# Sparse attention with a gated unit behind it: dummy matmuls at the start, a bias loaded as rows, score strips by query halves, and a new order of work

## The chip, the cores and the metric

The kernel runs on one core of a Trainium2 chip. The core has five engines that work through queues of their own, in order: TensorE (PE) multiplies, VectorE (DVE) and ScalarE (ACT) do element-wise work and read TensorE's results out of PSUM, GpSimd (POOL) does element-wise work in SBUF only and issues casting DMAs, and SyncE (SP) issues DMAs. The metric is the device time of one execution in microseconds (us); shown is the median of several runs.

## The reference

Inputs are q, k and v of shape (4 batches, 8 heads, 768 positions, 64), and the weights of a gated unit. For every head:

```python
k_min, k_max = k_chunks.min(3), k_chunks.max(3)          # 24 chunks of 32 keys
ub = sum(maximum(q * k_min, q * k_max))                  # a bound per query and chunk
ub = where(causal, ub, -1e9)
top_chunks = argsort(ub)[..., -6:]                       # six chunks per query
scores = where(selected and causal, (q @ k.T) / 8, -1e9)
attn = softmax(scores) @ v
```

The heads of a batch are put side by side as x (768 x 512), and then:

```python
h = relu(x @ w_in);  u, v = h[:, :512], h[:, 512:]       # w_in: 512 x 1024
v_n = (v - mean(v)) / sqrt(var(v) + 1e-6)                # over the 512 features
v_s = w_spatial @ v_n + b_spatial[:, None]               # over the 768 positions
out = (u * v_s) @ w_out                                  # w_out: 512 x 512
```

## The kernel before

**Tiling.** Two heads make a pair; there are 16 pairs, four to a batch. Positions come in six tiles of 128. Data is fp16, sums in PSUM are fp32. Eight PSUM tiles of 128 x 512 fp32 (`bank0` to `bank7`) serve all matmuls.

**A pair's preparation** (`prep_ops`, and `prep_first` for pair 0, which goes head by head). Keys (`kp`) and queries (`qs`) are loaded by position; a load casts from fp32 to fp16 on the way when POOL issues it (L370), or goes to a `stage` tile by SP (L376) and is cast by an engine. Keys are transposed to `kT` by TensorE (L440, L545) or by a DMA that transposes (L443). VectorE reduces `kT` to the chunk maxima and negated minima `kmm` (L449 to L455, L552 to L560); these are spread to `km`, and the keys to `kh`. Queries are transposed on TensorE (L477, L579), and their positive and negative parts go to `rq`. The bounds are matmuls of `rq` with `km` (L489, L590); VectorE adds the causal mask, takes the eight largest (`max`), and writes into free columns of `qs` whether a chunk lies below the sixth (`select`). Transposing `qs` once more (TensorE L525 and L616, or DMA L516) gives `a`: 64 rows of queries and 24 rows of marks. Below the keys in `kh` stand 24 rows of -30000 (copies of `ex`), so that one matmul gives scores with the unselected chunks suppressed.

**A pair's attention** (`attend_ops`). For each head the scores stand with keys on partitions and queries along the row; the 21 causal blocks of 128 x 128 are put into six strips, groups of up to 512 columns (`STRIPS`). A strip is one or two matmuls (L641) into a PSUM tile, and ScalarE takes its exponential into `e` (L651). On the six diagonal blocks the triangle is cut off, either by a matmul that adds -30000 (L644) ahead of the exponential, or on GpSimd by two selects over three blocks each (L659) after it. Then 21 matmuls of 65 columns with the values and a column of ones (L667), a reciprocal (L675) and a product (L679) into `x16`, and a transposition of `x16` to `xT` (TensorE L694, or a DMA issued at L688).

**The gated unit of a batch** (`mlp_ops`). For each of six position tiles: v (L713), its statistics and normalization `vn`; u (L740); the spatial product (L754), which VectorE joins with the bias column `bcol` and with u to g (L758); g's transposition `gT` (TensorE L768, or DMA L762); the output product (L775), a copy to `o`, and a store by SP (L780). The bias column is loaded at L347 straight into the shape of 128 partitions x 6.

**What sets the order.** Every operation is registered with its choices of engine and with what it reads and writes, and then a written plan is played (`Schedule.run`): a string in which three characters stand for one operation, two for its number and one for the engine chosen and for the PSUM tile taken. So the order within each engine's queue, the engine of every copy, and the tile of every matmul are all fixed by that string. Where an operation exists in two forms (transposition by TensorE or by DMA, triangle by TensorE or GpSimd, load by POOL or by way of a stage), the plan lists only one of them. Buffers go round in rings (four tiles `e`, eleven `vraw`, four `o`, eight `stage`).

Of the kernel before, what the change touches and what calls it, by code (L numbers as in the profile page):

```python
# [10 lines left out]
Alu = mybir.AluOpType  # L11
# [9 lines left out]

STRIPS = [
    [(0, 0, 512, 0)],
    [(1, 128, 512, 0)],
    [(2, 256, 512, 0)],
    [(0, 512, 256, 0), (4, 512, 256, 256)],
    [(1, 640, 128, 0), (3, 384, 384, 128)],
    [(5, 640, 128, 0)],
]
WIDTHS = [512, 512, 512, 512, 512, 128]  # L30
BASES = [0, 512, 1024, 1536, 2048, 2560]
EW = 2688
DIAGS = [(0, 512), (1792, 384)]


def blocks(groups):
    out = []
    for g in groups:
        for (t, q0, n, col) in STRIPS[g]:
            for j in range(n // P):  # L40
                out.append((t, q0 // P + j, BASES[g] + col + j * P))
    return out
# [19 lines left out]
    "9wSBv0By0A909e49f06k06L0Ao16uWC907IO78G9mCCC06M0Db09x0Ay09n0De05GKCB0CJ15H16m4CK16n0A0873S6+CDP0"
    "Gg0CL4CG2CF26v0A107906/0IA07J0CI0CE2CM1Dg0CH1700CN0ABK740Di07SWCD1Gl0CO8BG47K07T0750DS0Dd0Df07A0"
    "9jC090710AC0BDOCP0720BH08/0CQ09k07cS9pG7B0Jg07d0BeKBE09q06w4Bf0CR0760GwC7e0AV0B887C07NO7fG6x0B90"
    "7707U0BJKBK07O0Bb4Bc0CS0Dh0AD07L0Gx0Dl29g0Dn1Dj2B2SB307D07g07h07P1Dr8Go07iWDk10Y0BTKDs09r0BQCBR0"
    "9h4BhOBi07j0Dt0A20B5S7Q0BW87V0Dq1Dm0DuG7E07k19s09t0Gz09u07F0Dv07W0A3CAE0Dw0IF0Dp1CmOAF0BU07R0Do1"
    "CjKB60Dx07M07G0II0G/0CYW7rSBX0Cn0IS0D84Ck0AG07l87m0DV0H71BL0CbO7s0BA0CpKCZ07oWBj07n0CeG7H0H91DB8"
    "Cc07X07Y0DC07t07p0Dy0HA1Cf0Cq0BBOBM0BY0AICHB87q07b0H10CwSB/08MGHC07uKH81AJ17Z0BZWG+07a00Z0Bk0Jy0"
    "8N0H00BN0Jo07v0H20HD1Bl0H60BO0D5CD90H317w07x0Cx0D08IU0H40Cz4EGS82OH50If1Cg0Bm0Cr0D60D10E8CC+0D20"
    "HEKHF0E908O0Ih8LA0HG0EH0E548CWE60IW08D0Ij1HH0E2C8E0EWSE30Jl0Ii0IT0EJ4EK0Ig18F0EeKIV0Ef0Ch8EQCED4"  # L70
    "EhWDD0HI0EE0Cs08P0BoKIY0830IX0EX0OW0Ct0840Ib0ETG8W4ER0J+0IZ0EbSEU0Ia1Ic1Ei0Id2Ec0K00850Bp1D3CDE0"
    "Jz0DF0IkGIl0LQW8X07y0EA0EBOJ/0DG0Im0K208Q0EL0EM0KBSIn0LI08Y0Cu0Ie1LR1EN0860K108gCKC1EO0HZKLU0Io0"
    "8h0Ha0HsWHt0DIGEY0Hm8Hn08i0Ej0EZOKA1HUKEk0I1WHV0LF0K50RW0LT0KD1DJ1K718Z0Ev8Ob0K42I20K61K928a0K30"
    "El0Em0LV07/4OmKLW0HcOEoS8j0LY0Hd0Gr0Ep0K81HpGLX0Lc0KEC8TWE+SHfOE/0On0Ew0Oq0FIKHq0IL0F00FJ0Lb0Ex0"
    "Oe0KF08U0KG0FDGF10800FE0Op0LhSFK0JR8HOWHg0Ey0HR4EqKHP0Er0HS0F20J3OKH0JUCH+WIu4FF1La0Es1Q00JJGJ40"
    "Ez0FVKKI0Et0JV0Hh0810Iv0FW0H/0Li0Ld1JS0FX0FbOFc0Lj0LZ0HxCHu0Hy0Eu0Q80JX4JK0FL0Os0Ou0JY0IxSOr0LkW"
    "Iy08d8FG0FhKLe18G0Fi0Lf0J9CJA0Ll0Ot0Jr0F30JMGF84HW0F90J6SLg1JN0Lm0HXCHi0Ow2T00I30Fj1FA1HvGJGKFH0"
    "Hj08e0Ln0Ov2FB0F40F50K+8QI0I40J70JZ0Rb0P14P20P30Hk0Oy1Fd0I+W8JSJH0O/189OO+1Lo0Oz18A1K/0FC0P01Ro0"
    "FM0F60Ox0I508K0Re0JO0I/0KcKL18Kp4KmSL20J00Kd0P4CFYWKq0I60Kf8KxOFZ0FSKP50Kn0KO4Fa1FT0FeGKy0KP08k0"
    "KRSQ50P60P70JB0KZOJPWF70FU08B0Ja0Jb0Kg0FN0Ka0Jc0Ks4MGKFO0L+8Kt0KS0FkCFf0Fg0MROLuWMS0J14FQ0MH0JC0"  # L80
    "KUSFP0Fl0M9GGCOFR0LxKGD0KV0Ku0QU1P80QJ0L/0Kh0QV1Fm0I70LL0QK0MUSKW0JD0MM8Rp0JE0Rq0Fn0GE0MA0L30Lv0"
    "QL0MN0QM0QN0Fo0GF0Rr0Rs0MV0MX4MY0Jd0M3GQT1MZ0M6WFuCKv8L40KXSL50T50M70PE4PF0QO0PfOFv0MJWL60Fw0Ly0"
    "Fx0Rt0M40Oh08n88o1Fy0QX4Ki0Kj0PiKS02QZ0GMGMK0M00QY1PSCPPWQQ0QP1GN0QW1Kk0M18Pg0PT0T80PV4PW0Ru0TI0"
    "PHOPI0PtSQS0MB0GO0MC0MD0ME08L0L70PqCPK4Pu0QR1Pj0GP0MO0MPOMa0PL0GWSRx2QaKPn8G24Pr0Rw2M+GPcCMb0Po0"
    "Pd0Mc0Md0Pv0N8OGX0GY0S18Qb0G30G40Qc0Qd0S30TK0TV18V0Rv2Pk0Qe0PQ0Ry1GZ0FrCRh0MlKFs0TJ0S20TXWTY0MqS"
    "S48MgCM/0TM0S50TL0S60TZ1R/2Mh0N00TN0S70QB0TO0TP0TS0Mm0Mn1Mo0Mi0N90NA1F/WNXGPX0NY08p0S80GG0Qq8TU2"
    "TQ1G00Mp0QnCG50Mj0Qr0Mr0GQ0TR0Ms0QyKQz0PlWG10TaOTb0Qk8Mt0Tc0Td0Q/4Pw0Px0Mu0NZ0TT1TE0NLSQo0PM0Mk0"
    "NIKN3GN40N51N60Ql0RCCRD0NJ0R+2N70RN8RO0NK1G60R00NM0QvONN0PNCQs0Mv0PY0Py0Qw0SfGGJ8Sg0St4Su0ScSNUK"
    "GK1R6OGa0Rz0Te0Sd0N10NV0NRWNS0GL0TF0Mw0My0R70TC0SKGR10Ft0PZ0Pa0SP8SS4SQ0SL0SnSSo0NW1NOONP0SECSF0"
    "RK8NQ1RHGR9KQtSNB0RI0R20GTOSiCR30N20RA0Mx0R40SqGRL0GdKRE0NC0Sr0ND0Sj0RP0G98ST0GU18f0NE0Ge1TnSTo0"  # L90
    "GA0SVGMz0NF0RFOTqCOMKTW1U64SW0SHSSI0NT1RQ0Tr0Na8SM0Nb0TkGTl0Ts0UCWTySU70NkCUD0Nl0NG0Sk0NH0Pz0Nc0"
    "U9GTz0Sv0T/4RR0RS0Nm0UA0UNOSX0Nn0NuWRT0Nd0No0U00SNSSY0SZ0TD0UKGUL0UO0Ne0UH4SlCSw0Sa0Nv0Tv8O2GUI0"
    "UP0Sx0Sy0Tw0Sz0ON0OO0U10Nw0TtOVNSU20U30U40Gf0UE0UF4UQ0UR0US0Nx0Ny0NrCNs0OP0UW8O30UUOUg4UV1UqCUvW"
    "O40Uh0O50UbKU+OUi1U/0V00Uj0Uk0UX0VBGV10V20Nt0UY0Uc0UZ0GB0Uw0Ux1VH4VI0Ud0Ue0Ur0Us0Uf0Ua0Ut0Uu0Uy0"
    "VJ0VKOUl0VO0Um0VP0OC8NhKUz0O60Ni0V8WUn0N/CUo0OQ0V30V40V60V90OD0GV0V70V50VL0O94OA1VC0OB0VuSVQKOE0"
    "VE4O00VA0O10Up0Vv0VR0VS0OF0VT0OTCVD0VM0VaWVb0Vc0Vd0Nj0Vw0VkGOG0VF0Vl0Vx0OU0Vm0VU0OV0Ve0OJOVG1Vn0"
    "W28W30Vy0W40WCKWD0WE0VhCW50WF0OK0Vo0OL0VXWW60WHSV/4Vi0WI0Vj0VrGVY0W00VZ0W10Vs0Vt0WJOWK0WL0W98WA0"
    "WB0"
# [3 lines left out]
class Bank:  # L102
    def __init__(self, cls):
        self.cls, self.tile = cls, None
# [14 lines left out]
class Schedule:  # L119
# [3 lines left out]
    def __init__(self, banks, caps):  # L123
        self.ops, self.banks, self.caps = [], banks, caps
        self.keys, self.mode = {}, {}

    def op(self, alts, emit, key, r=(), w=(), take=None, drop=None, load=0.0, tag="", when=None, after=()):
# [66 lines left out]
def kernel(  # L194
# [39 lines left out]
    pp = ctx.enter_context(tc.psum_pool(name="psum", bufs=1))  # L234
    banks = [pp.tile([P, 512], F32, name=f"bank{j}") for j in range(8)]
    s = Schedule(banks, {"sc": 3, "tr": 2, "ub": 1, "av": 2, "mlp": 4})
# [34 lines left out]
    bcol = cp.tile([P, NQT], F32, name="bcol")  # L271
    w_in_sb = cp.tile([P, NDO, DFF], F16, name="w_in")
# [7 lines left out]
    stage_r = ring(8, [P, NQT, D], F32, "stage")  # L280
# [10 lines left out]
    e_r = ring(4, [P, EW], F16, "e")  # L291
    rec_r = ring(4, [P, NQT, 1], F32, "rec")
    x_r = ring(3, [P, NQT, 2, D], F16, "x16")
    xT_r = ring(3, [P, NDO, S], F16, "xT")
    vr_r = ring(11, [P, DH], F32, "vraw")
# [7 lines left out]
    o_r = ring(4, [P, DM], F32, "o")  # L303

    nc.scalar.preload_act_table_set("natural_log_exp_and_others")
# [9 lines left out]

    def preset(qs):
        nc.vector.memset(qs[:, :, 0, 0:D], 0.0)
        nc.vector.memset(qs[:, :, 1, D:P], 0.0)

    def const_ops():  # L320
        s.op(("DVE", 0.1, 0.2), lambda: nc.vector.memset(identity, 0.0), -100, w=["identity"])
        s.op(("POOL", *pool(P)), c_identity, -100.95, w=["identity"], r=["identity"])
        for j in range(2):
            s.op(("DVE", 0.1, 0.2), lambda j=j: nc.vector.memset(km0[j], 0.0), -96 + j, w=[("km0z", j)])
# [298 lines left out]
    def attend_ops(i, key):  # L623
# [3 lines left out]
        for hi in range(2):  # L627
# [6 lines left out]
            for part in range(2):  # L634
                for g in range(3 * part, 3 * part + 3):
                    bs = Bank("sc")

                    def score(g=g, bs=bs, hi=hi, af=af, tri=False):
                        for (t, q0, n, col) in STRIPS[g]:
# [3 lines left out]
                            if dg:  # L643
                                mm(bs.f32[:, col:col + P], lhsT=identity, rhs=tri_t, start=False, stop=True)  # L644
# [185 lines left out]
```

## Time and profile before

| | |
|---|---|
| median of 6 runs | 196.69 us (196.08 to 198.28) |
| profiled execution | 196.08 us, of which the span from first to last instruction is 194.1 us |
| granted TensorE clock | 0.998 |
| TensorE matmuls | 1888, busy 180.8 us (93% of the span) |
| VectorE, ScalarE, GpSimd busy | 159.1, 147.7, 118.3 us |
| exponentials (L651) | 192, of which 160 have 512 columns (613 ns each) and 32 have 128 (298 ns) |
| triangles on GpSimd (L659) / TensorE (L644) | 48, 552 ns each / 48 matmuls |
| DMA | 29.5 MB, 122457 packets |

A row of the profile names a line of the kernel, an engine, an operation, what it writes and reads, how often, its busy time and its mean length. An arrow in brackets names what ended the idle time ahead of it. In the rows by stretches, each engine's busy time is followed by its number of instructions, and after the engines come the granted clock, the DMA engines' share and GB/s. Matmuls overlap in a pipeline, so a busy TensorE isn't one at its highest rate.

### The profile page before, as it was taken

The page shows a single profiled execution, that of the slowest core. Times are in us where ns is not written, and L with a number is a line of the kernel's source. Part 1 is how long each engine was busy: PE and PEld are TensorE (multiplying, and loading weights), DVE is VectorE, ACT ScalarE, POOL GpSimd, SP SyncE. Part 2 cuts the span into 40 slices and gives each one's busy share as a digit, 9 for nine tenths or more (in the row PEclk, how much of TensorE's full clock was granted, in tenths as well). Part 3 has the DMA queues.
Part 4 walks back from the last instruction along what each step waited for, and adds up shares of the span by engine and source line. Part 5 has one row for each costly group of instructions (what it writes and reads, how often), then busy time and mean ns, then how long its engine had stood idle before and what let it go on. Part 6 is the DMA issues. An engine that isn't in the chain of part 4 may idle for free.

```text
span 194.1 us, 5292 instructions
## 1 busy us (share of the span) xinstructions
PE 180.8 (93%) x1888; PEld 112.8 (58%) x1888; DVE 159.1 (82%) x568; ACT 147.7 (76%) x317; POOL 118.3 (61%) x207
## 2 busy tenths in 40 slices
PE   0579999999997999999999999999999999999992
PEld 0367888885664656565566566555565664444440
DVE  8799999997999789998999986799889436983620
ACT  7799999999996999778989978667888722652142
POOL 8699999999999798697976785523213530000000
PEclk9999999999999999999999999999999999999999
DMA  6999999999999999999999999799793264406565
GB/s 140 136 158 167 190 164 153 148 141 171 155 155 170 133 105 164 134 156 137 214 163 151 194 105 156 186 140 215 154 258 71 41 149 137 109 0 198 139 204 216
DMA packets 122457, 29.50 MB, mean 152 GB/s; under 512 B 117056, under 2 KB 119360, under 8 KB 122432
## 3 DMA queue, kind: packets, MB, share of 16 engines
q0 software_dynamic: 72528, 11.60, 93.5%
q1 hardware_dynamic: 49904, 17.57, 46.5%
q8 instruction: 14, 0.23, 0.5%
q14 instruction: 11, 0.09, 0.2%
HBM read 24.38 MB, written 6.29 MB: 158 GB/s over the span
## 4 chain that ended last, share of the span: by engine, by line
PE 73%; ACT 10%; DVE 7%; DMA 6%; issue 1%; SPq 1%; ACTq 0%; DVEq 0%
PE bank L641 15%; PE bank L754 13%; PE bank L775 10%; PE bank L740 9%; PE bank L667 9%; PE bank L713 8%; ACT e L651 4%; DMA a<-qs 4%; DMA stage<-in_k_dram 2%; PE bank L477 2%; ACT rq L250 1%; PE bank L489 1%; ACT kT L240 1%; PE bank L694 1%; ACT kh L240 1%
## 5 line engine op out<-in xcount | busy, mean ns | idle before, releaser
L651 ACT ACTIVATE e<-bank 128x512 f16<-128x512 f32 (+1 forms) x192 | 92.3, 561 | 12.6 <-PE bank L641 10.2
L641 PE MATMUL bank<-a,kh 128*128 128x512 f16 (+3 forms) x256 | 56.1, 305 | 1.1 <-DMA a<-qs 1.0
L659 POOL TENSOR_SCALAR_AFFINE_SELECT e<-e 128x384 f16<-128x384 f16 x48 | 25.7, 552 | 22.5 <-ACT e L651 21.5
L754 PE MATMUL bank<-vn,wsT 128*128 128x512 f16 x144 | 38.0, 379 | 0.0
L641 PEld LDWEIGHTS <-kh 128*128 128x128 f16 x256 | 22.7, 98 | 16.2 <-DMA a<-qs 1.2
L667 PEld LDWEIGHTS <-e 128*128 128x128 f16 x672 | 25.4, 97 | 5.0 <-issue 0.3
L667 PE MATMUL bank<-vt,e 128*128 128x65 f16 x672 | 27.1, 193 | 0.2 <-ACT e L651 0.2
L740 PE MATMUL bank<-w_in,xT 128*128 128x512 f16 x96 | 25.9, 379 | 0.0
L242 POOL COPY kh<-kT 64x384 f16<-64x384 f16 x46 | 24.0, 521 | 3.2 <-PE bank L641 1.3
L758 DVE SCALAR_TENSOR_TENSOR g<-bank,bcol,u 128x512 f16<-128x512 f32 x24 | 17.6, 745 | 10.1 <-PE bank L754 9.9
L370 POOL DMA_DIRECT2D qs<-in_q_dram x30 | 25.0, 836 | 0.0
L713 PE MATMUL bank<-w_in,xT 128*128 128x512 f16 x96 | 24.4, 379 | 0.0
L240 ACT COPY o<-bank 128x512 f32<-128x512 f32 x18 | 10.4, 587 | 18.3 <-PE bank L775 18.3
L775 PE MATMUL bank<-w_out,gT 128*128 128x512 f16 x96 | 23.6, 379 | 0.0
L754 PEld LDWEIGHTS <-wsT 128*128 128x128 f16 x144 | 13.4, 98 | 12.1
L679 DVE TENSOR_TENSOR x<-bank,rec 128x384 f16<-128x384 f32 x32 | 17.4, 547 | 0.4
L370 POOL DMA_DIRECT2D kp<-in_k_dram x15 | 15.5, 1032 | 2.1 <-ACT qs L240 1.5
L719 DVE BATCH_NORM_STATS2 st<-vraw 128x6 f32<-128x512 f32 x24 | 16.3, 684 | 0.4
L370 POOL DMA_DIRECT2D vt<-in_v_dram x15 | 15.4, 1025 | 0.0
L775 PEld LDWEIGHTS <-gT 128*128 128x128 f16 x96 | 9.1, 98 | 9.8
L713 PEld LDWEIGHTS <-xT 128*128 128x128 f16 x96 | 9.0, 98 | 9.0
L740 PEld LDWEIGHTS <-xT 128*128 128x128 f16 x96 | 8.9, 98 | 8.5
(90 smaller groups left out, 280.2 us busy)
## 6 DMA issues: line engine op xcount, KB each, us to landing
out_dram<-o SPq DMA_DIRECT2D x24, 256.0 KB, 2.3
kp<-in_k_dram POOLq DMA_DIRECT2D x15, 192.0 KB, 6.4
qs<-in_q_dram POOLq DMA_DIRECT2D x30, 96.0 KB, 5.6
vt<-in_v_dram POOLq DMA_DIRECT2D x15, 192.0 KB, 6.5
ws_raw<-in_moe_w_spatial_dram POOLq DMA_DIRECT2D x3, 384.0 KB, 6.2
w_in<-in_moe_w_in_dram POOLq DMA_DIRECT2D x4, 256.0 KB, 7.3
w_out<-in_moe_w_out_dram POOLq DMA_DIRECT2D x2, 256.0 KB, 6.0
stage<-in_k_dram SPq DMA_DIRECT2D x2, 192.0 KB, 3.4
```

Of the source, the lines that this page charges most:

```text
L242: nc.gpsimd.tensor_copy(o, f)
L370: s.op(("POOL", cost, 0), lambda: nc.gpsimd.dma_start(out=o[0] if len(o) == 1 else o[2], in_=f[0] if len(f) == 1 else f[2]), key, w=w, loa ...
L641: mm(bs.f32[:, col:col + n], lhsT=kh[:, hi, t * P:(t + 1) * P], rhs=af[:, q0 // P:(q0 + n) // P, :], start=True, stop=not dg)
L651: s.op(("ACT", *act_cost(WIDTHS[g])), lambda g=g, bs=bs, e=e: nc.scalar.activation(out=e[:, BASES[g]:BASES[g] + WIDTHS[g]], in_=bs.f32[:, ...
L659: nc.gpsimd.affine_select(out=o, in_=o, compare_op=Alu.is_ge, fill=0.0, base=0, channel_multiplier=-1, pattern=[[0, 3], [1, P]])
L667: mm(o[:, qi, :], lhsT=e[:, c:c + P], rhs=vt[:, hi, t, 0:D + 1], start=(part == 0 and n == 0), stop=(part == 1 and n == len(bl) - 1))
L679: nc.vector.tensor_tensor(x16[:, :, hi, :], in0=o[:, :, 0:D], in1=rec.to_broadcast([P, NQT, D]), op=Alu.mult)
L713: mm(bk.f32, lhsT=x[:, ko, t * P:(t + 1) * P], rhs=w_in_sb[:, ko, DH:DFF], start=(ko == 0), stop=(ko == NDO - 1))
L740: mm(bk.f32, lhsT=x[:, ko, t * P:(t + 1) * P], rhs=w_in_sb[:, ko, 0:DH], start=(ko == 0), stop=(ko == NDO - 1))
L754: mm(bk.f32, lhsT=wsT[:, si, t * P:(t + 1) * P], rhs=vn[:, si, :], start=(si == 0), stop=(si == NQT - 1))
L758: s.op(("DVE", 0.67, 0.80), lambda t=t, bk=bk, g=g: nc.vector.scalar_tensor_tensor(out=g, in0=bk.f32, scalar=bcol[:, t:t + 1], in1=u_r[nu[ ...
L775: mm(bo.f32, lhsT=gT[:, db, :], rhs=w_out_sb[:, db, :], start=(db == 0), stop=(db == KO - 1))
```

## The change

- **Dummy matmuls.** A zeroed tile `warm` is multiplied with itself in four groups (31, 5, 5 and 5 matmuls of 128 columns). The groups stand in the plan ahead of, and between, the key and query transpositions of pair 0.
- **Spatial bias.** The vector is loaded as six rows of 128 (`braw`), transposed on TensorE with a small fp32 identity `idf`, and copied to `bcol`.
- **Score strips.** The six groups hold the same 21 blocks but are ordered by query halves: two groups for the queries 0 to 383, four for 384 to 767. Each half has its own `e` tile (768 and 1920 columns, rings of four). A group now has one to three matmuls, 12 per head where there were 8. The values are multiplied after a half's groups: 6 blocks, then 15.
- **Triangles.** Each half's three diagonal blocks are cut on GpSimd as before or on VectorE, by a minimum with a 0/60000 tile `tri_m`. TensorE remains as a choice.
- **Loads.** Only k and q of pair 0 may go by way of a stage. The plan uses that for the first head's k and q.
- **Rings.** `vraw` nine, `o` three, `stage` four, `rec` eight.
- **PSUM.** Eight single tiles, as before (`double` is None). A variant that splits whole pairs into halves is written but set to zero (`SPLIT = 0`).
- **The plan** is a new string. Before / after it runs: key transpositions on TensorE 12 / 13 (of 17, pair 0's two heads counted apart); `a` on TensorE 10 / 10; x 7 / 6; g 1 / 5; triangles of eight heads on TensorE in both; the other 48 on GpSimd 48 / 40, on VectorE 0 / 8.

```diff
 STRIPS = [
-    [(0, 0, 512, 0)],
-    [(1, 128, 512, 0)],
-    [(2, 256, 512, 0)],
-    [(0, 512, 256, 0), (4, 512, 256, 256)],
-    [(1, 640, 128, 0), (3, 384, 384, 128)],
-    [(5, 640, 128, 0)],
+    [(0, 0, 256, 0), (2, 256, 128, 256), (0, 256, 128, 384)],
+    [(1, 128, 256, 0)],
+    [(0, 384, 384, 0), (5, 640, 128, 384)],
+    [(1, 384, 384, 0), (4, 512, 128, 384)],
+    [(2, 384, 384, 0), (3, 384, 128, 384)],
+    [(3, 512, 256, 0), (4, 640, 128, 256)],
 ]
-WIDTHS = [512, 512, 512, 512, 512, 128]
-BASES = [0, 512, 1024, 1536, 2048, 2560]
-EW = 2688
-DIAGS = [(0, 512), (1792, 384)]
+HALF = [(0, 2), (2, 6)]
+WIDTHS = [512, 256, 512, 512, 512, 384]
+BASES = [0, 512, 0, 512, 1024, 1536]
+EW = [768, 1920]
+DIAGS = [(0, 256), (384, 512)]
...
-    stage_r = ring(8, [P, NQT, D], F32, "stage")
+    stage_r = ring(4, [P, NQT, D], F32, "stage")
...
-    e_r = ring(4, [P, EW], F16, "e")
-    rec_r = ring(4, [P, NQT, 1], F32, "rec")
+    e_r = [ring(4, [P, n], F16, f"e{h}_") for h, n in enumerate(EW)]
+    rec_r = ring(8, [P, NQT, 1], F32, "rec")
...
-    vr_r = ring(11, [P, DH], F32, "vraw")
+    vr_r = ring(9, [P, DH], F32, "vraw")
...
-    o_r = ring(4, [P, DM], F32, "o")
+    o_r = ring(3, [P, DM], F32, "o")
...
+        s.op(("DVE", 0.08, 0.15), lambda: nc.vector.memset(warm, 0.0), -102, w=["warm"])
+        for j in range(NWARM):
+            bw = Bank("tr")
+
+            def spin(n=31 if j == 0 else 5, bw=bw):
+                for _ in range(n):
+                    nc.tensor.matmul(bw.f32[:, 0:P], lhsT=warm, rhs=warm, start=True, stop=True)
...
+        s.op(("DVE", 0.13, 0.25), lambda: nc.vector.tensor_scalar(
+            tri_m, in0=tri_t, scalar1=0.0, scalar2=60000.0, op0=Alu.is_ge, op1=Alu.mult), -30, r=["tri"], w=["trim"])
...
-        s.op(("SP", 0.45, 2.5), lambda: nc.sync.dma_start(out=bcol, in_=moe_b_spatial.rearrange("(t p) -> p t", p=P)),
-             20, w=["bcol"])
+        s.op(("SP", 0.45, 0), lambda: nc.sync.dma_start(out=braw, in_=moe_b_spatial.rearrange("(t p) -> t p", p=P)),
+             -60, w=["braw"], load=0.1, tag="lb")
...
+        s.op(("PE", 0.25, 0.47), lambda: nc.tensor.transpose(bb.f32[:, 0:NQT], braw, idf), 20, r=["braw", "idf"], w=[bb], take=bb)
...
-            cast, stage = s.choice(("ld", name, i))
+            cast = None
+            if i == 0 and name != "v":
+                cast, stage = s.choice(("ld", name, i))
...
+                def tri(eng, c0=c0, st=st, e=e):
                     o = bass.AP(e.tensor, e.offset + c0, [list(e.ap[0]), [st, 3], [1, P]])
-                    nc.gpsimd.affine_select(out=o, in_=o, compare_op=Alu.is_ge, fill=0.0, base=0,
-                                            channel_multiplier=-1, pattern=[[0, 3], [1, P]])
+                    if eng == "DVE":
+                        nc.vector.tensor_tensor(o, in0=o, in1=tri_m.unsqueeze(1).to_broadcast([P, 3, P]), op=Alu.min)
+                    else:
+                        nc.gpsimd.affine_select(out=o, in_=o, compare_op=Alu.is_ge, fill=0.0, base=0,
+                                                channel_multiplier=-1, pattern=[[0, 3], [1, P]])
```

## The prediction

> **What bounds the kernel now.** I read the page's totals and slices, then stretches of the run, the timeline of the start, the chain that ended last, and the groups by shape. From the page:
>
> ```profile
> PE 180.8 (93%) x1888; PEld 112.8 (58%) x1888; DVE 159.1 (82%) x568; ACT 147.7 (76%) x317; POOL 118.3 (61%) x207
> ...
> PE   0579999999997999999999999999999999999992
> ```
>
> TensorE (PE) has gaps only in the first three slices (4.9 us each), in one slice near 60 us and at the end. Busy time counts overlapped latencies, so I take TensorE's demand from dense pieces of the chain (start, length, work, count):
>
> ```profile
> 28.29 0.34 PE bank L525 x6
> ...
> 153.80 0.65 PE bank L667 x21
> ...
> 182.43 2.59 PE bank L754 x12
> ```
>
> That is 56 ns per 128-column transposition, 31 ns per 65-column matmul with the values, 216 ns per 512-column matmul. Priced so, the 1888 matmuls need: gated unit 432 x 216 = 93.3; scores 32 heads x 2688 columns = 36.5; values 672 x 31 = 20.8; 310 transpositions 17.4; 48 triangles 2.7; 170 small bound matmuls 4.3; together 175 us. The last matmul ends at 190.5, so 15.5 us are lost. Before 16.0 us only 60 transpositions and 20 bound matmuls ran, 3.9 us at these rates: 12.1 us are lost there. The other 3.4 lie later: 1.2 between 16 and 24 us, and then one visible stall plus about 1.1 in small pieces.
>
> The start, by stretches (length, then busy us of PE, PEld, DVE, ACT, POOL):
>
> ```profile
> 4.00:6.00 2.00, 0.50 (x3) 0.24 (x3) 1.65 (x6) 0.57 (x2) 1.92 (x3) 1.00 1.46 192
> 6.00:8.00 2.00, 1.32 (x9) 0.79 (x9) 1.10 (x7) 1.96 (x5) 0.59 (x1) 1.00 1.94 106
> 8.00:16.00 8.00, 6.35 (x69) 5.72 (x70) 7.66 (x43) 7.78 (x17) 7.91 (x11) 1.00 2.09 163
> 16.00:24.00 8.00, 7.78 (x116) 6.19 (x115) 7.58 (x41) 8.00 (x17) 7.57 (x18) 1.00 1.83 178
> ```
>
> From 8 us VectorE (DVE) and ScalarE (ACT) are full; TensorE waits for them. Only around 5 to 7 us do both have holes: they wait for the second head's keys. The timeline shows that, and the one later stall:
>
> ```profile
> 5.79 0.51 ACT L240 CAST kp<-stage 128x384 f16<-128x384 f32 x1 [1.43 <-DMA stage<-in_k_dram]
> ...
> 6.89 0.36 DVE L244 COPY kT<-bank 128x384 f16<-128x384 f16 x1 [1.14 <-PE bank L545]
> ...
> 7.15 0.82 PE L579 MATMUL bank<-identity,qs 128*128 128x128 f16 x6 [0.29 <-ACT qs L240]
> ...
> 17.11 1.08 ACT L651 ACTIVATE e<-bank 128x512 f16<-128x512 f32 x2
> ```
>
> ```profile
> 59.35 0.83 PE L641 MATMUL bank<-a,kh 128*128 128x128 f16 x5 [1.04 <-DMA a<-qs]
> ```
>
> The first exponential starts at 17.11. At 59.35 scores of pair 5 waited for their transposition by DMA, which the chain shows as 7.22 us long.
>
> [...] six transpositions took 0.82 us at 7.15 and pace at 0.34 later. [...] The column bias load agrees: 3 KB held SP's queue for 1.10 us and took 5.6 us to land.
>
> **The change part by part.** The plan string can be read by hand with Schedule.run's rule (two characters number the operation, the third gives engine and bank); counts below come from that.
>
> Dummy matmuls: 31 + 5 + 5 + 5 of 128 columns, cold at some 105 ns (six transpositions in 0.82 us, one lasting 0.31). The first 36 run from about 1.05 to 4.9 us, where TensorE has nothing else; the cast of k0 ended at 4.36, so they delay the first transposition by up to 0.5 us, which VectorE's queue covers (below). They may bring full speed by about 5 us, so a step of six transpositions ends some 0.3 us sooner; three such steps are in the first pair's chain. Later gaps may cool the array again: worth 0 to 0.9, inside the ramp below.
>
> Loads: k1 and q1 of pair 0 move from SP to POOL's casting queue; SP's two other stages, and a value load of pair 15, go. A new wait: in TensorE's queue the second head's key transposition waits for k1, and behind it stand the first head's queries, pair 1's keys and everything after. k1's issue follows the identity on POOL, at about 1.46. The shortest staged landing gives 3.05 us (0.80 to 3.85), the median key load before 16 us gives 6.1: it lands between 4.5 and 7.6. I take 6.0, since it is half as large and first in its queue; before, the staged one came at 5.79.
>
> The ramp, walked with the rows' durations: from ex (ends 2.1) VectorE has presets, memsets and three ex copies, 3.6 us, ahead of the first key copy, so that starts at 5.75 and finds its input. Reductions, second key copy (7.3 to 7.7), its reductions, pair 1's key copy, the queries' positive and negative parts (rq) follow without a hole: bounds at 10.4, select at 12.4. ScalarE is then in its own queue (copies, rq parts, key halves) and copies the first head's a at 13.5 to 14.3; four small copies and a key copy (0.8 + 0.8) stand before the first exponential, at 15.9. Before: 17.11, so 1.2 sooner; the second head's a, on VectorE, ends 16.3 against 17.2, 0.9 sooner. Work queued on ScalarE and VectorE ahead of TensorE's tenth us of work is equal in both plans (about 20 and 23.5 us), so the lead lasts: minus 1.0. Bounds: 0 (k1 late, or ScalarE's extra copies ahead of pair 2) to minus 2.5 (VectorE has 2 us less ahead of TensorE's twelfth us).
>
> Bias rows: SP's 1.10 becomes about 0.5; one small transposition, one copy of six columns: 0.1 us on engines; free, hidden by the bound chain; without cover 0.1.
>
> Score strips: the same 2688 columns per head and six exponentials, ScalarE's columns unchanged, but 12 matmuls instead of 8: 128 more x 2.7 ns = 0.35 us on TensorE, all on the path. Values are taken after two groups, then four; same 21 matmuls.
>
> Triangles: the same eight heads keep theirs on TensorE (48). Of 48 on GpSimd 8 move to VectorE, priced by the nearest row, a 128x384 f16 minimum over keys, 421 ns: 3.4 us there, 4.4 off GpSimd. VectorE's queue after 24 us has slack only in total (it is 97% busy to 44 us), but the first moved one is pair 4's. I take 0; 0 to 0.5.
>
> Re-planned transpositions: five gated tiles on TensorE instead of one, 4 x 4 x 56 = 0.9 us; keys 13 instead of 12, x 6 instead of 7: nothing. TensorE's sum: 0.35 + 0.9 + 0.05 = plus 1.3.
>
> The stall at 59: between pair 5's select and its first score the old plan leaves 7.2 us of TensorE work, the new one 9.1; against 7.22 us for the transfer that removes the stall: minus 1.3 (1.04 shown idle and the slower pieces at its sides). Next late is the shortest other distance: pair 13's 5.5 us, where before 5.4 ran without a stall; I take 0 for new ones, 0 to 1.5. Smaller rings (vraw 9, o 3): the last stores land 2.3 us after issue, and the plan keeps 4.7 us between tiles that share a buffer: 0, up to 0.3. "Eight PSUM tiles" is what was there. The end is again three output tiles, a copy and a store.
>
> Sum: -1.0 - 1.3 + 1.3 = -1.0. Profiled execution 196.08 (span 194.1, 1.98 around it) becomes 195.1; the median of the runs lies 0.6 above it, so 195.7. A measurement of this kernel can tell about 1% from no change.
>
> **The rivals.** Warm ramp in full: VectorE's hole and its 2 us of deferred work both count, -2.5; and the longer distances remove 0.7 of the small losses: 196.7 - 2.5 - 1.3 - 0.7 + 1.3 = 193.5. For: all transposition distances grew at the low end; against: ScalarE, as full as VectorE, has nothing less to do.
>
> Late second head (slower): k1 by POOL lands at 7.6 instead of 6.0. TensorE's queue is in order, so bounds and scores of both heads come 1.3 us later than before instead of 1.0 sooner; and a new late transfer takes back the stall (0 instead of -1.3): 196.7 + 1.3 + 1.3 = 199.3. It decides once k1 lands later than about 7.0. For: loads took 6.1 us here; against: those were twice as large and behind four staged loads.
>
> No warming: the array stays cold until dense work begins; the ramp gains 0.5 only: 196.2.
>
> **How the numbers follow.** Chances: forecast 0.38 (spread 1 us), no warming 0.10, warm ramp 0.33, late head 0.19. Faster by over 1% (below 194.7): 0.33 and 0.06 of the forecast's spread, 0.39; slower (above 198.7): 0.19; within 1%: 0.42. The range 193.0 to 199.0 leaves out the lower part of the warm ramp (0.08) and the upper of the late head (0.12).
>
> **What would show it.** Right: the first exponential near 16 us; 0.34 us paces for six transpositions by 7 us; no DVE hole at 5 to 7; no wait on the a transposition near 59; 1.3 us more TensorE work. Wrong: TensorE waiting on kp after 7 us, a ScalarE-bound stretch to 30 us with more loss than 1.2, or a new DMA wait in the middle.

## The result, and the profile after

The changed kernel takes 195.9 us in the median of 35 runs (194.6 to 198.5), beside 197.2 us of the kernel before on the same chips: a ratio of 0.9946, with an interval of 0.9927 to 0.9966. The forecast was 195.7 us and "within 1%". The profiled execution took 195.07 us, of which the span is 193.3.

The page of the kernel after, totals (busy time, share of the span, instructions), TensorE's slices and its granted clock:

```profile
PE 185.1 (96%) x2079; PEld 124.7 (65%) x2079; DVE 160.8 (83%) x575; ACT 149.8 (77%) x326; POOL 115.6 (60%) x198
...
PE   7689999899999999999999999999999999999992
...
PEclk9969999999999999999999999999999999999999
```

The dip of before at 59 us is gone, and the first slice is full, of dummies. The third digit of the clock is new: the granted clock was 0.50 from 10.44 to 13.86 us, most of that slice.

I price TensorE's matmuls much as in the prediction: columns / 2.4 plus 2.7 ns, the straight line through its measured 216 ns at 512 columns and 56 at 128 (these are from start to start; one such matmul lasts 379 and 219 ns in the profile); 30 ns for the 65 columns of a value matmul and 25.5 ns for a bound matmul, their paces in the profile; dummies at nothing. "Loss" at time T is T less the demand of all matmuls started by then. The demand is 175.7 us, before 174.4. The table says where the loss arises, in single profiled executions of both kernels and of all experiments below.

```
us lost by   16 us   24    36    56    60   100   180
before        11.9  12.9  13.0  13.2  14.5  15.3  15.8
after         10.8  11.8  12.7  12.8  12.8  13.5  13.6
e1_no_dummies 10.5  11.7  14.0  16.5  16.6  18.3  18.6
e2            11.9  13.3  13.2  13.4  14.9  15.9  16.2
e3            12.0  13.6  13.6  14.1  15.0  20.5  22.8
e4            10.7  11.6  12.6  12.6  12.7  13.2  13.6
e5            11.4  12.1  12.2  12.3  12.5  15.9  16.0
e6            11.0  12.1  12.3  12.3  12.3  13.0  13.2
e7            10.4  12.0  12.4  13.0  13.1  13.7  14.1
e9            10.2  11.2  11.4  11.4  12.4  12.7  13.0
e10           10.7  11.4  11.6  12.0  12.5  13.2  14.1
e11           11.1  12.1  12.2  13.4  13.3  14.7  14.9
e12           12.1  13.8  13.8  13.8  13.8  15.8  17.9
e15           10.7  11.4  13.5  13.4  13.5  16.1  16.2
```

So the kernel after is 1.1 us ahead at 16 us, gives back 0.6 by 56, gains 1.2 at 59, and 0.4 in small pieces after that: 2.1 us less lost at 180 us, 2.0 at the end, 1.27 us more to do, 0.8 us in all (span 194.1 to 193.3). Some executions of every kernel are slower than the rest: the medians given are of all executions, the ratios leave the slow ones out, and the profiles of e1 and e3 are of slow ones.

The timeline of the start, after (start, length, engine, line, work, count; in brackets the idle time ahead and what ended it):

```profile
1.05 4.02 PE L337 MATMUL bank<-warm 128*128 128x128 f16 x36 [1.05 <-DVE warm L331]
...
5.72 0.53 PE L573 MATMUL bank<-identity,kp 128*128 128x128 f16 x3
6.04 0.85 PE L607 MATMUL bank<-identity,qs 128*128 128x128 f16 x6
8.21 0.51 PE L468 MATMUL bank<-identity,kp 128*128 128x128 f16 x6 [1.32 <-DMA kp<-in_k_dram]
...
11.43 0.80 PE L468 MATMUL bank<-identity,kp 128*128 128x128 f16 x6
...
13.91 0.50 PE L644 MATMUL bank<-identity,qs 128*128 128x128 f16 x6
```

```profile
5.66 0.34 DVE L247 COPY kT<-bank 128x384 f16<-128x384 f16 x1
```

```profile
15.44 0.96 ACT L683 ACTIVATE e<-bank 128x384 f16<-128x384 f32 x2
```

The second head's keys (5.72) made TensorE wait for nothing, and VectorE's first key copy is at 5.66; the first exponential starts at 15.44, before at 17.11. Six transpositions took 0.85 us at 6.04, 0.51 at 8.21, 0.80 again at 11.43 and 0.50 from 13.91. The dummies bought full speed late, and it was lost again.

The waits of the kernel after, the longer ones on DMAs (total in us, times, longest), and TensorE's timeline at the second:

```profile
PE bank L468 <- DMA kp<-in_k_dram: 1.3, 1, 1.3
...
ACT o L243 <- DMA out_dram<-o: 0.9, 1, 0.9
PEld L703 <- DMA vt<-in_v_dram: 0.8, 1, 0.8
PE bank L703 <- DMA vt<-in_v_dram: 0.6, 1, 0.6
```

```profile
34.75 0.83 PE L703 MATMUL bank<-vt,e 128*128 128x65 f16 x21 [0.58 <-DMA vt<-in_v_dram]
```

```profile
59.50 1.00 PE L703 MATMUL bank<-vt,e 128*128 128x65 f16 x27
```

No wait on `a<-qs` is left at 59. A new one stands at 34.75, where pair 2's values are late. POOL's queue issues the two value loads at 25.93 together, 1 us each, and in the new plan pair 3's goes ahead of pair 2's. The wait on the store is ScalarE's, near the end; TensorE lost nothing by it.

### The profile page after: what moved, and what is told of

Same layout as the page of the kernel before. It is cut to its first block, busy times and chain, and to the rows that moved or that the text cites. A ratio compares the mean times of both kernels' runs of the same rounds, so it can differ in the third digit from the quotient of the medians.

```text
span 193.3 us, 5676 instructions
## 1 busy us (share of the span) xinstructions
PE 185.1 (96%) x2079; PEld 124.7 (65%) x2079; DVE 160.8 (83%) x575; ACT 149.8 (77%) x326; POOL 115.6 (60%) x198
## 4 chain that ended last, share of the span: by engine, by line
PE 71%; ACT 7%; DVE 7%; DMA 7%; POOL 5%; issue 1%; ACTq 0%; DVEq 0%; POOLq 0%
PE bank L793 16%; PE bank L672 13%; PE bank L814 11%; PE bank L703 9%; PE bank L779 8%; PE bank L752 8%; DMA vt<-in_v_dram 4%; ACT e L683 4%; DMA kp<-in_k_dram 3%; PE bank L505 2%; POOL kh L245 1%; PE bank L468 1%; DVE st L758 1%; PE bank L517 1%; POOL kp L398 1%
## 5 line engine op out<-in xcount | busy, mean ns | idle before, releaser
L683 ACT ACTIVATE e<-bank 128x512 f16<-128x512 f32 (+2 forms) x192 | 92.6, 560 | 13.5 <-PE bank L672 11.7
L672 PE MATMUL bank<-a,kh 128*128 128x128 f16 (+2 forms) x384 | 57.3, 259 | 0.4 <-ACT e L683 0.4
L672 PEld LDWEIGHTS <-kh 128*128 128x128 f16 x384 | 32.2, 98 | 15.5 <-issue 0.5
L694 POOL TENSOR_SCALAR_AFFINE_SELECT e<-e 128x384 f16<-128x384 f16 x40 | 21.6, 546 | 29.1 <-ACT e L683 28.1
L793 PE MATMUL bank<-vn,wsT 128*128 128x512 f16 x144 | 37.1, 379 | 0.0
L398 POOL DMA_DIRECT2D qs<-in_q_dram x31 | 26.0, 844 | 0.3 <-issue 0.2
L758 DVE BATCH_NORM_STATS2 st<-vraw 128x6 f32<-128x512 f32 x24 | 15.9, 681 | 2.1 <-ACT vraw L253 1.8
L398 POOL DMA_DIRECT2D vt<-in_v_dram x16 | 16.5, 1034 | 0.0
L398 POOL DMA_DIRECT2D kp<-in_k_dram x16 | 16.4, 1026 | 0.0
L769 DVE TENSOR_SCALAR vn<-vraw,mv,rs 128x512 f16<-128x512 f32 x24 | 14.5, 626 | 0.6 <-ACT rs L765 0.6
L752 PEld LDWEIGHTS <-xT 128*128 128x128 f16 x96 | 8.8, 98 | 8.3
```

Source lines behind the costliest of these rows:

```text
L398: s.op(("POOL", cost, 0), lambda: nc.gpsimd.dma_start(out=o[0] if len(o) == 1 else o[2], in_=f[0] if len(f) == 1 else f[2]), key, w=w, loa ...
L672: mm(bs.f32[:, col:col + n], lhsT=kh[:, hi, t * P:(t + 1) * P], rhs=a[:, f // P:(f + n) // P, hi, :], start=True, stop=not on)
L683: s.op(("ACT", *act_cost(n)), lambda g=g, n=n, bs=bs, e=e: nc.scalar.activation(out=e[:, BASES[g]:BASES[g] + n], in_=bs.f32[:, 0:n], func= ...
L694: nc.gpsimd.affine_select(out=o, in_=o, compare_op=Alu.is_ge, fill=0.0, base=0, channel_multiplier=-1, pattern=[[0, 3], [1, P]])
L752: mm(bk.f32, lhsT=x[:, ko, t * P:(t + 1) * P], rhs=w_in_sb[:, ko, DH:DFF], start=(ko == 0), stop=(ko == NDO - 1))
L758: s.op(("DVE", 0.60, 0.74), lambda vraw=vraw, st=st: nc.vector.bn_stats(st, vraw), kk, r=[("vr", nvr[t])], w=[("st", nst)])
```

## The experiments

Three batches of four; the kernels of a batch ran on one chip, with the kernel before among them. The first batch holds e1 to e4, the second e5, e6, e9 and e12, the third e7, e10, e11 and e15. Ratios are to the kernel before of the same batch.

### The dummies alone, taken out and put in

```diff
 # e1_no_dummies: the kernel after
-                for _ in range(n):
+                for _ in range(0):
 # e2_before_dummies: the kernel before; warm is a zeroed part of wsT
+                for _ in range(5 if hi else 36):      # ahead of a head's key transpositions
+                    mm(bk.f32[:, 256:384], lhsT=warm, rhs=warm, start=True, stop=True)
+                for _ in range(0 if hi else 5):       # ahead of the first head's query transpositions
+                    mm(bq.f32[:, 384:512], lhsT=warm, rhs=warm, start=True, stop=True)
```

> The changed kernel without its 46 dummy matmuls, all else in place. If the dummies carry the ramp (the array warm from 7.0 us on gives the lead): TensorE's loss by 16 us (time minus what the matmuls so far need at full rate) goes from 10.8 back to about 11.9, as in the kernel before, the first exponential from 15.4 to 16.5, the time up by 1.0 us, ratio to the kernel before near 1.000. If the new order and loads carry it: the loss by 16 us stays within 0.4 of 10.8 (the first key transposition even starts up to 1 us earlier, since it no longer stands behind 36 dummies), time within 0.4 us of the changed kernel, ratio 0.993 to 0.997.

> The kernel before with the same dummies alone: 36 ahead of the first head's key transposition, 5 ahead of the second's, 5 ahead of the first head's queries. If dummies carry the ramp: loss by 16 us from 11.9 to about 10.9, ratio 0.994 to 0.996. If the order does: VectorE and ScalarE still wait for the second head's keys at 5.8 us, loss by 16 us 11.5 to 12.0, ratio 0.998 to 1.001.

Measured: without them 195.86 us, 0.9962 (0.9935 to 0.9988), beside 0.9946 with them; the kernel before with them 195.91 us, 0.9970 (0.9944 to 0.9996). So the medians put what the dummies give at 0.3 and 0.6 us; the intervals don't tell 0.3 from nothing, and in the kernel before they allow up to 1.1. The second ratio lies between what the two theories of e2 had expected. But the loss by 16 us goes with the order of work, not with the dummies: 10.5 with the new order and no dummies, 11.9 with the old order and dummies. In e2 the array was fast from 4.5 us until 14, which the old order didn't use:

```profile
4.49 0.34 PE L551 MATMUL bank<-identity,kp 128*128 128x128 f16 x3
...
6.10 0.34 PE L551 MATMUL bank<-identity,kp 128*128 128x128 f16 x3 [0.99 <-ACT kp L240]
6.89 0.51 PE L587 MATMUL bank<-identity,qs 128*128 128x128 f16 x6 [0.45 <-ACT qs L240]
8.32 0.51 PE L444 MATMUL bank<-identity,kp 128*128 128x128 f16 x6 [0.92 <-DMA kp<-in_k_dram]
```

TensorE takes 0.34 and 0.51 us in place of 0.50 and 0.82, and waits the longer for casts and keys.

### Warm all through against cold all through

Both kernels here load pair 2's values first (next experiment). One has no dummies; the other has the 46 and 32 more.

```diff
 # e7_hold_warm
+            for _ in range(16 if i == 1 else 0):      # ahead of pair 1's key transpositions
+                mm(bk.f32[:, 384:512], lhsT=warm, rhs=warm, start=True, stop=True)
...
+                for _ in range(10 if hi else 6):      # ahead of pair 0's bounds
+                    mm(bu.f32[:, 256:384], lhsT=warm, rhs=warm, start=True, stop=True)
 # e11_values_first_no_dummies
-                for _ in range(n):
+                for _ in range(0):
```

> The kernel with pair 2's values loaded first, plus 32 more dummy matmuls (16 ahead of pair 1's key transpositions, 6 and 10 ahead of the first pair's two groups of bound matmuls), so that TensorE has no long rest between 8 and 14 us, where it ran at half clock in the kernel after. If the half clock costs the ramp: groups of six transpositions near 11.5 us take 0.5 instead of 0.8 us, the loss by 16 us falls from 10.7 to 10.2-10.5 us, and the ratio is 0.001 to 0.003 below the run with values first alone. If the ramp is held by ScalarE, VectorE and the landings of the keys: the clock is held and the first exponential stays at 15.4 us, and the ratio is that of the run with values first, within 0.002.

> The kernel with pair 2's values loaded first, without the 46 dummy matmuls. If the dummies are worth nothing, as in the run without them and in the kernel before with them added: loss by 16 us 10.5 to 11.0 us, ratio that of the run with values first within 0.002. If they are worth something that the wait for pair 2's values hid: 0.5 to 1.0 us more, ratio 0.991 to 0.994.

Measured: 0.9897 (0.9856 to 0.9937) and 0.9915 (0.9871 to 0.9959). TensorE's and ScalarE's timeline, first of the warm kernel, then of the cold one:

```profile
10.95 0.49 PE L470 MATMUL bank<-identity,kp 128*128 128x128 f16 x6
11.29 0.50 PE L648 MATMUL bank<-identity,qs 128*128 128x128 f16 x6
...
12.94 0.51 PE L470 MATMUL bank<-identity,kp 128*128 128x128 f16 x6 [0.82 <-DMA kp<-in_k_dram]
```

```profile
12.70 0.79 ACT L243 COPY a<-bank 128x768 f16<-128x768 f16 x1
...
14.99 0.96 ACT L687 ACTIVATE e<-bank 128x384 f16<-128x384 f32 x2
```

```profile
10.98 0.80 PE L468 MATMUL bank<-identity,kp 128*128 128x128 f16 x6
11.57 0.85 PE L644 MATMUL bank<-identity,qs 128*128 128x128 f16 x6
...
12.85 0.85 PE L468 MATMUL bank<-identity,kp 128*128 128x128 f16 x6
```

```profile
12.70 0.79 ACT L243 COPY a<-bank 128x768 f16<-128x768 f16 x1
...
15.00 0.96 ACT L683 ACTIVATE e<-bank 128x384 f16<-128x384 f32 x2
```

This is the clearest reading of the study. One array ran at full speed from 4.3 us (groups of six transpositions start 0.33 us apart at 11 us), the other at half speed until 15.4 (0.64 apart at 12 us; six took 0.85 us at 13.49 and 0.52 at 15.42), and ScalarE copied `a` at 12.70 in both and began the exponentials at 14.99 and 15.00. The warm one led by 0.7 us of TensorE's work at 16 us, and had 0.1 of it left at 24. The clock of the array is not what holds the ramp in these two. ScalarE is busy for 3.8 to 4.0 of every 4 us from 8 to 24 us in both. The other profiles agree: in e1, e4, e5, e9, e10 and e15, whatever their clock, the first exponential starts between 14.8 and 15.03 us, where ScalarE had at most 0.3 us of idle time from 4.4 us on; it is later in the two profiles in which ScalarE waited longer for VectorE (15.44 in the kernel after with 0.6 us, 15.62 in e6 with 1.0). The ratios of the warm and the cold kernel differ by 0.4 us, inside their intervals; as in e1 and e2 the kernel with dummies is the faster, so a gain of this size is neither shown nor excluded.

### Pair 2's values first, and later still

In the plan `520` is the load of pair 3's values and `3k0` that of pair 2's.

```diff
 # e4_values_first
-    "4901w08i05G13508h14iO4k05204CW5O02J03k05P01x00a04E05H14a84c02K04QS8U02u42w05Q04FG8T03NO4H03b03c0"
+    "4901w08i05G13508h14iO4k03k04CW5O02J05205P01x00a04E05H14a84c02K04QS8U02u42w05Q04FG8T03NO4H03b03c0"
 # e15_values_later
+    "4901w08i05G13508h14iO4k05204CW5O02J05P01x00a03k04E05H14a84c02K04QS8U02u42w05Q04FG8T03NO4H03b03c0"
```

> The changed kernel with two loads exchanged on GpSimd's queue: the values of pair 2 ahead of those of pair 3. If the wait for pair 2's values at 34 us is a real loss: the idle of 0.6 there goes, the loss between 32 and 36 us falls from 0.75 to under 0.2, the time by 0.5 to 0.8 us, ratio to the kernel before 0.990 to 0.992. If TensorE was held there by ScalarE and VectorE as well: the wait moves to an exponential or to the values of pair 3, the time stays, ratio 0.994 to 0.996.

> The kernel after with pair 2's values issued one step later still, behind the second half of the input weights, so some 0.7 us later. If TensorE's wait for them sets the time, as the run with values first says: the wait of the last matmuls on the values near 34 us grows from 0.6 to 1.3 us or more, the loss at 36 us by as much, and the ratio is 0.998 to 1.002. If the gain of the run with values first came from elsewhere (pair 3's values or the keys changed landings): the ratio stays at 0.995, within 0.002.

Measured: values first 194.31 us (six runs, 194.0 to 194.9), 0.9858 (0.9809 to 0.9908); later 195.82 us, 0.9943 (0.9915 to 0.9971). The wait for the values is gone from the waits of the first, and longer in the second:

```profile
PE bank L703 <- DMA vt<-in_v_dram: 1.8, 1, 1.8
```

That is 1.8 us against 0.6, and the loss at 36 us is 13.5 against 12.7: in the profiled executions the delay acts as expected. The medians don't follow: e15 is no slower than the kernel after (0.9946), where the expectation for a wait that sets the time had 0.998 or more, and its profiled execution was one of its slowest, 197.6 us. And the profiled execution of e4 has the span of the kernel after's, 193.2 against 193.3, since pair 5's keys took back the gain (0.68 us at 29.59). What stands is a difference of groups: six kernels with pair 2's values first and the rest of the plan kept, but for small edits, lie at 0.986 to 0.992 (e4, e6, e7, e9, e10, e11), three with pair 3's first at 0.994 to 0.996 (the kernel after, e1, e15). Within batches it is 1.5 us (e4 against e1) and 0.4 to 0.8 us (e7, e10 and e11 against e15). So this order of two loads is worth about 1 us. The ten profiles of the new order say where: with pair 3's values first, TensorE waits for values between 34 and 37 us in all three (0.58, 1.79 and, in e1, 2.89 us), and the loss grows by 0.9 to 2.3 us from 24 to 36; with pair 2's first it waits for them in none of seven (e5 included), and in six of these the loss grows by 0.1 to 0.4 (by 1.0 in e4, whose keys were late). How much a us of delay costs in the medians is not settled, as e15 shows. e4 is the fastest kernel of its batch, and its ratio lies below that of the kernel after.

### The second head's keys late

```diff
 # e6_late_head: values first, and pair 1's keys (2N0) issued on POOL ahead of pair 0's second-head keys
-    03G 0m0 0G0 080 0T1 0r1 0M0 0W0 1FK 0B0 2N0 0s0
+    03G 2N0 0m0 0G0 080 0T1 0r1 0M0 0W0 1FK 0B0 0s0
```

> As e4_values_first, but on GpSimd's queue the keys of pair 0's second head stand behind pair 1's keys, so they are issued 1.0 us later. If the second head's keys decide the ramp (the rival of the prediction): the loss by 16 us rises from 10.7 to 11.7 or more, the time by 1 us, ratio 0.990 to 0.992. If pair 1's keys, for which TensorE waits at 8.2 us, or ScalarE's and VectorE's queues decide: the loss stays within 0.4 of 10.7, ratio 0.985 to 0.988.

Measured: 194.56 us, 0.9901 (0.9863 to 0.9940). TensorE's timeline has the rival of the prediction, and what follows it:

```profile
7.19 0.34 PE L573 MATMUL bank<-identity,kp 128*128 128x128 f16 x3 [1.26 <-DMA kp<-in_k_dram]
7.37 0.50 PE L607 MATMUL bank<-identity,qs 128*128 128x128 f16 x6
7.70 0.50 PE L468 MATMUL bank<-identity,kp 128*128 128x128 f16 x6
```

TensorE waits 1.26 us for the second head at 7.19, but then not for pair 1 (1.32 us at 8.21 in the kernel after): one wait takes the other's place. The first exponential starts at 15.62, in e4 at 15.03; the loss at 24 us is 12.1 against 11.6. The median is 0.26 us above that of e9, the other kernel of its batch with this order of loads, and the intervals overlap. I had priced a late second head at 2.3 us against the forecast's ramp.

### The stall at 59 us alone

```diff
 # e12_before_later_scores: the kernel before; pair 6's first scores behind four more u matmul groups
   (the plan's triples, in order)
-    Dp1 CmO AF0 BU0 7R0 Do1 CjK B60 Dx0 7M0 7G0 II0 G/0 CYW 7rS BX0 Cn0 IS0 D84 Ck0 AG0 7l8 7m0 DV0 H71 BL0 CbO 7s0
+    Dp1 AF0 BU0 7R0 Do1 B60 Dx0 7M0 7G0 II0 G/0 7rS BX0 IS0 AG0 7l8 7m0 7s0 CmO CjK CYW D84 Cn0 Ck0 DV0 H71 BL0 CbO
```

> The kernel before with one edit of its plan: four matmul groups of the gated unit (u of tiles 5 and 3) ahead of the first scores of pair 6, so that TensorE has 1.7 us more to do until pair 6's transposition has landed. If that wait is a loss of its own: the step of 1.24 us between 56 and 60 us goes to under 0.3, ratio 0.990 to 0.994, so this alone is as much as the whole change gained. If ScalarE and VectorE hold TensorE there anyway: the loss moves on to the next scores, ratio 0.997 to 1.000.

Measured: 197.17 us, 1.0013 (0.9981 to 1.0046): nothing gained. TensorE doesn't wait for the transposition at 59 any more. Its timeline and ScalarE's around there, and TensorE's later:

```profile
58.79 1.89 PE L740 MATMUL bank<-w_in,xT 128*128 128x512 f16 x8
60.52 1.83 PE L641 MATMUL bank<-a,kh 128*128 128x128 f16 x9
62.62 0.38 PE L740 MATMUL bank<-w_in,xT 128*128 128x512 f16 x1 [0.27 <-ACT e L651]
```

```profile
60.99 1.57 ACT L651 ACTIVATE e<-bank 128x512 f16<-128x512 f32 x3 [1.92 <-PE bank L641]
```

```profile
134.20 0.60 PE L641 MATMUL bank<-a,kh 128*128 128x512 f16 x2 [1.55 <-DMA a<-qs]
```

The loss between 56 and 60 us falls from 1.24 to 0.05, but 1.05 comes back from 60 to 64: while TensorE did gated work in place of the scores, ScalarE ran dry for 1.92 us (before, 1.41 at the same place), and then the nine score matmuls stretched over 1.83 us and TensorE waited for an exponential. Another transposition is late at 134. Filling TensorE's wait with other work left ScalarE the same scores too late. In the kernel after, where other scores stand in between, ScalarE has no idle time above 0.3 us between 54 and 66.

### Twelve score matmuls in the old order

```diff
 # e3_before_split: the kernel before
-    [(0, 0, 512, 0)],
-    [(1, 128, 512, 0)],
-    [(2, 256, 512, 0)],
-    [(0, 512, 256, 0), (4, 512, 256, 256)],
+    [(0, 0, 384, 0), (0, 384, 128, 384)],
+    [(1, 128, 384, 0), (1, 512, 128, 384)],
+    [(2, 256, 384, 0), (2, 640, 128, 384)],
+    [(0, 512, 128, 0), (0, 640, 128, 128), (4, 512, 256, 256)],
```

> The kernel before with 12 score matmuls per head in place of 8, in the same six groups and columns (the 512-column ones cut to 384 + 128, one of 256 to 128 + 128): 128 matmuls and weight loads more, the cost of the new strips by itself. By the fixed cost of a matmul, 2.7 ns each: 0.35 us, ratio 1.001 to 1.003, and no change of place of any wait. The rival, weight loads that are no longer hidden (98 ns each): up to 5 us or more, ratio above 1.01.

Measured: 199.16 us, 1.0127 (1.0090 to 1.0165), a ratio that only the rival had. But the weight loads stay hidden: the shapes keep their mean lengths (128 columns 220 ns, 384 columns 329 ns; 219 and 326 before), and from start to start score matmuls follow each other at 56 ns (128 columns) and 162 ns (384), as before. So the matmuls cost what was reckoned, 0.35 us of demand. What grew in the profiled execution is, in the waits of e3:

```profile
PE bank L641 <- DMA a<-qs: 5.3, 2, 3.6
...
PEld L440 <- DMA kp<-in_k_dram: 1.9, 3, 1.1
```

Before, the wait on `a<-qs` was 1.0 us. The longer of the two waits is again for pair 6's transposition, which took 9.76 us here and 7.22 before. But this execution took 203.1 us against a median of 199.2, so its amounts aren't those of the median. Where the 2.5 us of the medians sit, and whether the strips of the change cost as much in the new order, no run shows.

### Gated tiles, bias and triangles

All three stand on e4.

```diff
 # e5_g_by_dma: gated tiles 0.0, 0.2 and 3.1 by DMA, as in the old plan (here the first of them; 7T0 is the DMA)
-    IA0 H01 7U8 CK0 AW0 AX0 Gu0 7d0 DN0 By0 DJK 7V0 DK0
+    IA0 H01 7T0 CK0 AW0 AX0 Gu0 7d0 DN0 By0 DJK DK0
...
 # e9_bias_column
-        s.op(("SP", 0.45, 0), lambda: nc.sync.dma_start(out=braw, in_=moe_b_spatial.rearrange("(t p) -> t p", p=P)),
+        s.op(("SP", 0.45, 0), lambda: nc.sync.dma_start(out=bcol, in_=moe_b_spatial.rearrange("(t p) -> p t", p=P)),
...                                                    # and no idf, transposition or copy
 # e10_triangles_gpsimd: the eight triangles' triples; the last character is the engine, 1 VectorE, 0 GpSimd
-    9Y1 Ge1 Ha1 Iu1 P21 Q81 QM1 R41
+    9Y0 Ge0 Ha0 Iu0 P20 Q80 QM0 R40
```

> The changed kernel with pair 2's values loaded first (as e4_values_first, ratio 0.986) and with three of its five gated tiles transposed by DMA again (0.0, 0.2 and 3.1; 3.4 and 3.5 stay on TensorE). If TensorE's demand sets the time: 12 transpositions at 56 ns and no new wait, 0.7 us less than e4, ratio 0.982 to 0.984. If the transpositions on TensorE stood there because DMAs land too late: a wait for gT or for a later transposition on SP's queue appears, ratio 0.986 or above.

> As e4_values_first, but with the bias loaded straight into a column again, 768 elements of 4 bytes, third on SP's queue, and without its transposition and copy. If the rows are free and worth nothing: ratio within 0.002 of e4 (0.986), loss by 16 us 10.5 to 10.9. If the 768 small elements delay the loads of pair 1 (some 1000 packets a us move in the ramp): pair 1's keys land 0.5 to 0.8 us later, the loss by 16 us rises by as much, ratio 0.989 to 0.990.

> The kernel with pair 2's values loaded first, and the eight triangles that the change gave to VectorE back on GpSimd (48 of 48 there). If, as predicted, triangles cost nothing on either engine because no score or value matmul waits for one: within 0.002 of the run with values first (0.986 to 0.990). If GpSimd was late with them (about 0.55 us each, queued among its loads), TensorE's waits on e tiles rise from nothing by 0.3 to 1.0 us and the ratio is 0.988 to 0.994. If VectorE was the late one, the ratio falls by 0.002 to 0.003.

Measured: the gated tiles by DMA 197.47 us, 1.0015 (0.9969 to 1.0060); the bias as a column 194.30 us, 0.9897 (0.9846 to 0.9949); the triangles on GpSimd 195.43 us, 0.9914 (0.9881 to 0.9947). Only the first matters. It takes 12 transpositions, 0.67 us, from TensorE and makes the kernel slower by over 1% than the other two kernels of its batch with pair 2's values first (e6 and e9, both 0.990); in its timeline of VectorE and TensorE, and in its waits, stand:

```profile
76.66 0.75 DVE L797 SCALAR_TENSOR_TENSOR g<-bank,bcol,u 128x512 f16<-128x512 f32 x1 [2.68 <-DMA gT<-g]
```

```profile
77.47 0.38 PE L672 MATMUL bank<-a,kh 128*128 128x384 f16 x2 [1.63 <-DVE g L797]
```

```profile
ACT o L243 <- DMA out_dram<-o: 2.7, 1, 2.7
```

VectorE couldn't write the next g while a DMA still read the old one out of its buffer, and TensorE waited 1.63 us for the PSUM tile that this g was to free. The kernel after has neither, its wait for a store is 0.9, and e5's loss grows by 3.4 us from 60 to 100 us, where the kernel after's grows by 0.7. The rest of the plan was laid for transpositions on TensorE, so a plan made anew for the DMAs might lose less.

## Why the prediction was right, and where it was not

**The ramp, -1.0: right in size.** The profiles have -1.1 at 16 and at 24 us, in a profile whose first exponential is 0.4 us later than in most others of the new order. VectorE's walk held: first key copy 5.66 for 5.75, `a` copied by ScalarE at 13.14 for 13.5, first exponential 15.44 for 15.9. k1 came by 5.7 at the latest, where I had 6.0, so the late second head (chance 0.19) fell, and e6 suggests that its price was far too high.

**The dummies: the parenthesis failed, without harm.** "They may bring full speed by about 5 us" was an estimate that no view of before shows, and it was wrong in this execution, where six transpositions still took 0.85 us at 6.04; in e7 and e2 the first fast groups came at 4.3 and 4.5. That the array may get slow again holds: the granted clock was 0.50 from 12 to 14 us in e4, but 1.00 in e7, whose further dummies fill TensorE's gaps. The weight I gave to all this, nothing outside the ramp, was right, but two rivals were built on warmth: "no warming" (196.2) and, with VectorE's deferred work, "warm ramp in full" (193.5). In e7 and e11, warm and cold, the first exponential started at the same time to 0.01 us, so the clock gives neither a basis in the ramp. What in the new order gives the 1.1 us I have not taken apart further, and no run has the new order with the old strips: e6 accounts for at most 0.5 of it by the early second head, e9 for none by the bias.

**The stall at 59, -1.3: the time was right (-1.2), the pair and the account were not.** The scores at 59.35 are pair 6's, not pair 5's: the transposition for them was issued at 52.08 and took 7.22 us. Priced as above, 5.9 us of TensorE's work stood between the issue and these scores before, and 8.6 stand there after. The 7.2 of the prediction against a transfer of 7.22 would have left hardly a stall to remove. But e12 removed the stall too, and gained nothing. "Next late is the shortest other distance" looked for the next wait in the same list of transpositions and at TensorE alone. ScalarE's supply at 60 to 64 came next. From 56 to 64 us together, 1.3 us are lost before, 1.1 in e12 and 0.4 in the kernel after, so of the 1.3 forecast some 0.8 stays.

**TensorE's demand, +1.3: right** (1.27). e5 shows that three of the gated tiles, in this plan, are well spent on TensorE. For the strips' 0.35 the price per matmul was right; yet as many more matmuls cost 2.5 us in the old order (e3), which nothing in my sum could have given.

**"I take 0 for new ones": the step that failed.** The distances that I checked were those of the DMA transpositions. I didn't lay the loads' order in POOL's queue against the order of use; that would have shown pair 3's values ahead of pair 2's. The wait cost 0.6 us in the profiled execution, within my 0 to 1.5, and the order of those loads about 1 us in the medians.

**Free edits.** Triangles: eight took 2.8 us on VectorE (347 ns each; 421 were taken), and nobody waited; back on GpSimd TensorE waited once, 0.5 us, for one of them (e10), and the time is the same within the interval. The bias as rows held SP's queue for 0.47 us, as a column for 1.10, and is worth nothing that was seen (e9 0.9897, e6 0.9901). The smaller `o` ring brought ScalarE a wait of 0.9 us near the end, and TensorE none.

**The sum.** -1.1 - 1.2 + 1.27 + 0.6 - 0.4 is -0.8 in the profiles, for -1.0 forecast: the new wait, and small pieces after 60 us that I had only given to a rival, happen to cancel. That is luck, not the account.

## What to carry to other kernels

Before the clock of TensorE is warmed, see whether anything waits for TensorE in that stretch: here ScalarE was full, and a warm array mostly waited longer. After a re-plan, lay the order in which each queue issues its loads against the order in which they are used, queue by queue; one exchange of two loads was worth about as much as the whole change. A wait that is taken away is worth its length only if no other engine and no other transfer is due just behind it.

## What was not expected of the hardware

- **The same dummies brought full speed early or late.** The same 36 dummies from 1.05 us took 3.43 us in e7 and 4.02 in the kernel after, and the first fast group came at 4.3 and at 8.2 us. What makes this difference no run shows.
- **Busy time does not tell whether the speed is kept.** The kernel after, and then e7, from 8 to 16 us (bounds, length, busy us of PE, PEld, DVE, ACT, POOL, then the clock):

```profile
8.00:16.00 8.00, 6.81 (x95) 6.00 (x96) 6.94 (x34) 7.48 (x19) 7.95 (x11) 0.79 2.17 143
```

```profile
8.00:12.00 4.00, 3.26 (x60) 2.78 (x57) 3.83 (x23) 3.90 (x10) 4.00 (x7) 1.00 2.28 147
12.00:16.00 4.00, 2.96 (x47) 2.44 (x45) 3.54 (x18) 3.93 (x11) 3.91 (x6) 1.00 2.04 148
```

  TensorE was busy for 6.81 of these 8 us at a mean clock of 0.79 in the one, and for 6.22 at 1.00 in the other; the slow one is the busier in part because six transpositions take 0.85 us there and 0.50 at full speed. How much work keeps the speed was not measured.
- **The half clock comes back in nearly every execution.** The half clock from 10.44 to 13.86 us makes a mean granted clock of 0.991 in the profiled execution of the kernel after; 34 of its 36 executions on record have that or less, and all six of e4, which is as fast as any. The six of e7 have 0.997 to 1.000.
- **The clock digit is not the speed where TensorE has just begun.** In e11 the granted clock reads 1.00 from 8 to 14 us while six transpositions took 0.80 to 0.85 us. In the kernel after the first record of the clock is at 7.03 us, and the digit is 1.00 before it too, where six took 0.85 us at 6.04. The length of a known group is the better witness.
- **Landings scatter more than the edits under test.** Loads of 192 KB by POOL took 5.7, 7.8 and 8.9 us on chains of the kernel after and e4, against medians of 6.1 to 6.5. So a single wait of one profiled execution can differ by more than the medians do between kernels, and what it costs has to be read from several.
